# A linear-attention and squared-ReLU kernel: the planner's order replaced by a written table of steps

## The chip, the cores and the metric

One core of one Trainium2 chip runs the kernel. The metric is the device time of one execution in microseconds; below it is given as the median of three executions. The engines are TensorE (PE, with its weight loads PEld), VectorE (DVE), ScalarE (ACT), GpSimd (POOL) and SyncE (SP), which here only issues transfers.

## The reference

Four sequences (batch) of 768 tokens and 8 heads of 48 go through an attention with a decaying state, and its output, seen as 3072 tokens of 384, through two dense layers with a squared ReLU. r, k and v are 4 x 8 x 768 x 48, w and u 8 x 48, the weights 384 x 2048 and 2048 x 384, all in float32.

```python
for t in range(S):
    cur = np.einsum('bhd,bhe->bhde', u[None] * kt, vt)
    y[:, :, t] = np.einsum('bhd,bhde->bhe', rt, state + cur)
    state = w[None, :, :, None] * state + np.einsum('bhd,bhe->bhde', kt, vt)
...
h = np.maximum(x @ w_in, 0.0)
return (h * h @ w_out).astype(np.float32)
```

## The kernel before

The tokens are cut into 24 chunks of 128: chunk i is the piece i // 4 of sequence i % 4, so a state is handed on from chunk i to chunk i + 4. The work of a chunk is a chain of steps, and each step is one token of a list, such as `A12`. The engines run in the order of that list, each its own steps one after another. The steps of chunk i:

- `Lk`, `Lr`, `Lv` (SP, L593): the loads of k, r and v, 192 KB each, into eight buffers of each kind. `vb` (ACT, L635): v in bf16.
- `kh` (L606) and `rt` (L609): k and r times the powers of the decay, in bf16. `P0`, `P` (L614, L617), `du` (L621), `dv` (L631): the term with u. DVE or POOL run the products, `du` runs on DVE.
- The transposes of `kh` and `rt`: for the first chunks on PE (`Tk`, `Tr`, L641) with copies by ACT or DVE (`ek`, `er`, L602 and L603), for the later ones one transposing transfer `T` (SP, L662). `PE_T` is the first chunk that uses the transfer.
- `A` (PE, L672): the scores within the chunk, eight matmuls into two PSUM banks; `M` (DVE, L686): the mask, one instruction for each bank.
- `Y` (PE, L698 and L703): the output from the state and the masked scores; `U` (PE, L713) and `S` (DVE, L727 and L728): the new state; `xs` (DVE, L721): `Y` plus `dv`.
- The transpose of `xs`: on PE (`X`, L734) with a copy (`xT`) up to chunk `XD` - 1, from there a transposing transfer (`xT` on SP, L743).
- The dense layers work on units n, which are one chunk or a pair of chunks. `F` n_s (PE, L774): 12 matmuls of 128 columns for a single, 6 of 256 for a pair, into one bank; a single has four F steps, a pair eight. `R` (ACT, L787): ReLU out of PSUM. `Q` (L794 on ACT, L796 on POOL, L798 on DVE): the square; the one on DVE reads the bank once more, the others do not. `G` i_q (PE, L808): 4 matmuls of 384 columns, four G steps for a chunk. `os` (L819): the result out of PSUM; `st` (SP, L823): the store.
- The weights come in quarters, `W1_q` and `W2_q` (768 KB each, L758), with a cast `C1_q`, `C2_q` (L602) to bf16; `W2_3` comes by a transfer that POOL issues and that casts by itself (L760).
- At the start stand `wrow`, `urow` (loads of w and u), `ln`, `bw`, `exk`, `ext`, `bu`, `ub`, `wt`, `wl`, `wlm`, which make the powers of the decay and spread u over the partitions.

Every step of PE that takes a bank says which of the eight; a step that takes a bank again waits for the last reader of what lay in it. The `hr` tiles (R to Q) have four buffers, the `hq` tiles (Q to G) 32.

The order of the 915 steps comes from a planner, `make_plan` and `Plan.run`: every step has needs, costs by engine, a priority that follows from its due time with a period of 13 us for two chunks, and takes and gives banks. `run` plays them through with a model of the engines, of the transfer queues (`fluid`) and of the banks, always takes the step that can begin first, and writes down order, engine and bank. `MOVED` shifts single priorities by hand. At the end a loop walks through `order` and issues the steps; `plan.after` adds waits, such as a POOL step's wait for a DVE product that stands ahead of it.

Of the kernel before, what the change touches and what calls it, by code (L numbers as in the profile page):

```python
# [22 lines left out]
RING = 2.5
LANDING = 1.2
FILL = 8.0
FILL_GAP = 0.2
FILLED = False
FILL_UNTIL = 20.0
AHEAD = 2.8
TPA = 0.8  # L30
DVO = 0
MOVED = {
# [15 lines left out]
FLEX = 5
UB = -94.0
ST_SLACK = 5.0  # L50
W1GATE = [["Lv1"], ["Lv1"], ["Lv1"], ["Lv1"]]
W2GATE = [["Lv3"], ["Lk4"], ["Lv4"], ["Lk5"]]
HW1 = (0, 1, 2, 3)
HW2 = (0, 1, 2)
W1PRIO = (-93.5, -93.45, -92.4, -92.35)
W2PRIO = (-91.5, -91.4, -91.3, -91.2)
CASTS = ("ACT", "POOL")
XD = 18
WF = 5
LEAD = 3  # L60
SLACK = (1.0, 0.3, 0.5, 2.0)
LGATE = {6: ["W2_2"], 7: ["W2_3"]}
OPEN = {"kh": -6, "rt": 6, "P0": 8, "P": 10, "du": 4, "dv": 6, "S": 6}

# [9 lines left out]

class Plan:


    def __init__(self):
        self.steps = {}
        self.after = {}  # L80

    def add(self, key, eng, cost, needs=(), prio=0.0, lat=None, take=(), give=(), service=None,
            port=False, slack=0.0, ring=None, units=0.0):
        eng = (eng,) if isinstance(eng, str) else eng
        cost = cost if isinstance(cost, dict) else {e: cost for e in eng}
        self.steps[key] = dict(
            engs=eng, costs=cost, needs=[n for n in needs if n is not None],
            prio=prio + MOVED.get(key, 0.0),
            more=0.2 if lat is None else lat - max(cost.values()), take=take, give=give,
            service=service, port=port, slack=slack, ring=ring, units=units,  # L90
        )

    def fluid(self):
        key, queue, begin, service = self.jobs[-1]
        others = [self.span[j[0]][1] for j in self.jobs[:-1] if j[1] != queue]
        same = [self.span[j[0]][1] for j in self.jobs[:-1][::-1] if j[1] == queue][:1]
        begin = max([begin] + same)
        if not others or max(others) <= begin:
            self.span[key] = [begin, begin + service]
            return {key: self.span[key]}  # L100
        jobs = {q: [j for j in self.jobs if j[1] == q] for q in ("hw", "sw")}
        at = {"hw": 0, "sw": 0}
        left = {q: [j[3] for j in jobs[q]] for q in jobs}
        now = 0.0
        span = {}
        while any(at[q] < len(jobs[q]) for q in jobs):
            live = [q for q in jobs if at[q] < len(jobs[q]) and jobs[q][at[q]][2] <= now + 1e-9]
            coming = [jobs[q][at[q]][2] for q in jobs if at[q] < len(jobs[q]) and q not in live]
            if not live:
                now = min(coming)  # L110
                continue
            rate = {"hw": 1.0, "sw": 1.0} if len(live) == 1 else {"hw": 0.17, "sw": 0.83}
            step = min(left[q][at[q]] / rate[q] for q in live)
            if coming:
                step = min(step, min(coming) - now)
            for q in live:
                span.setdefault(jobs[q][at[q]][0], [now, now])
            now += step
            for q in live:
                left[q][at[q]] -= rate[q] * step  # L120
                if left[q][at[q]] <= 1e-9:
                    span[jobs[q][at[q]][0]][1] = now
                    at[q] += 1
        return span

    def room(self, at, units):

        spare = RING - units
        for key, q, _, _ in reversed(self.jobs):
            if q == "hw":  # L130
                a, b = self.span[key]
                u = self.steps[key]["units"]
                if u >= spare:
                    return max(at, b - (b - a) * spare / u)
                spare -= u
        return at

    def warm(self, at):
        return sum(max(0.0, b - max(a, at - 3.4)) for a, b in self.pe[-60:]) >= 2.0

    def fill(self, key, begin, end):

        if not self.steps[key]["take"] or begin > FILL_UNTIL:
            return 0, begin
        n = int(max(0.0, end - begin - FILL_GAP) * (FILL if begin > 4.0 else min(FILL, 4.5)))
        return n, self.dummies(n, begin)

    def dummies(self, n, begin):
        for _ in range(n):
            took = 0.107 if self.warm(begin) else 0.213  # L150
            self.pe.append((begin, begin + took))
            begin += took
        return begin

    def cost(self, key, eng, at):
        s = self.steps[key]
        c = s["costs"][eng]
        if eng == "PE" and not self.warm(at):
            c *= 1.75
        if s["port"] and eng == "DVE":  # L160
            c += max(0.0, self.free["POOL"] - at)
        if s["units"]:
            c = max(c, self.room(at + c, s["units"]) - at)
        return c

    def run(self, until=1e9):
        steps = self.steps
        free = self.free = {"SP": 0.5, "ACT": 1.8, "POOL": 2.8, "DVE": 1.5, "PE": 1.2}
        self.pe = []
        self.fills = {}  # L170
        self.jobs = []
        self.span = {}
        rings = {}
        done = self.done = {}
        self.start = {}
        self.took = {}
        self.eng = {}
        self.banks = {}
        bank_free = [0.0] * BANKS
        held = {}  # L180
        order = self.order = []
        caps = {"O": 4, "H": 4, "A": 5}
        lanes = []
        lock = None
        users = {}
        open_needs = {}
        for key, s in steps.items():
            open_needs[key] = len(set(s["needs"]))
            for n in set(s["needs"]):
                users.setdefault(n, []).append(key)  # L190
        place = {key: n for n, key in enumerate(steps)}
        todo = {key for key in steps if not open_needs[key]}
        while todo:
            taken = {b for h in held.values() for b in h[1]}
            spare = sorted((bank_free[b], b) for b in range(BANKS) if b not in taken)
            counts = {}
            for kind, banks in held.values():
                counts[kind] = counts.get(kind, 0) + len(banks)
            seen = {}
            for key in sorted(todo, key=place.get):  # L200
                s = steps[key]
                ready = max([done[n] for n in s["needs"]], default=0.0) + s["slack"]
                if s["take"]:
                    name, kind, count = s["take"]
                    if counts.get(kind, 0) + count > caps[kind]:
                        continue
# [680 lines left out]
```

## Time and profile before

| | us |
|---|---|
| median of three executions (176.71 to 177.4) | 176.97 |
| profiled execution | 176.04 |
| its span, first to last instruction | 174.0 |
| PE busy | 163.7 |
| PEld busy | 124.7 |
| DVE busy | 128.7 |
| ACT busy | 112.5 |
| POOL busy | 102.9 |

Busy times are sums over the span; the rest of an engine's span is waiting. A line of the chain of waits gives the start, the length and the work on which the end hung at that time; a line of the timeline gives start, length, engine, line, operation and tiles, and in brackets how long the engine had been idle and what released it. A landing time counts from the issue of a transfer to its completion.

### The profile page before, as it was taken

The numbers are of one execution on the slowest core, as the hardware profiler recorded it, in microseconds if no ns is written. First come the engines' busy times: TensorE is split into PE (matmuls) and PEld (weight loads), VectorE is DVE, ScalarE is ACT, GpSimd is POOL, SyncE is SP. The second block draws the span as 40 slices with busy tenths as digits, with TensorE's granted clock in tenths as the row PEclk, the third lists the DMA queues.
The fourth block names the chain that finished last, engine by engine and source line by source line (L and its number), as shares of the span: only waits on it lengthen the run. The fifth ranks groups of instructions, "written<-read, shape, count | busy, mean of one in ns | idle before, by whom it ended". The sixth has DMA issues, their size and how long they took to land.

```text
span 174.0 us, 4703 instructions
## 1 busy us (share of the span) xinstructions
PE 163.7 (94%) x1866; PEld 124.7 (72%) x1866; DVE 128.7 (74%) x238; ACT 112.5 (65%) x205; POOL 102.9 (59%) x121
## 2 busy tenths in 40 slices
PE   1979799999999999999999999999999999999992
PEld 1349688676887779967776867888776787866860
DVE  4698889589769499989699886999887269540620
ACT  4557899893795557946586743974784294743932
POOL 5022643249979998998999999969798200000000
PEclk9999999999999999999999999999999999999999
DMA  4999999999999799999799999999995621110302
GB/s 94 191 321 245 344 219 384 175 202 181 191 159 211 175 224 171 211 167 208 149 232 191 177 221 177 224 237 181 175 166 108 171 70 49 23 41 31 136 0 90
DMA packets 102520, 30.11 MB, mean 173 GB/s; under 512 B 95842, under 2 KB 100964, under 8 KB 102500
## 3 DMA queue, kind: packets, MB, share of 16 engines
q1 hardware_dynamic: 101972, 29.44, 84.6%
q0 software_dynamic: 528, 0.39, 1.8%
q8 instruction: 14, 0.23, 0.6%
q14 instruction: 6, 0.05, 0.1%
HBM read 20.45 MB, written 4.72 MB: 145 GB/s over the span
## 4 chain that ended last, share of the span: by engine, by line
PE 83%; DMA 8%; ACT 4%; SPq 3%; issue 1%; DVE 0%; ACTq 0%
PE ps_O L808 35%; PE ps_H L774 33%; DMA kf<-in_k_dram 5%; PE ps_A L672 4%; DMA vf<-in_v_dram 3%; PE ps_Y L703 2%; SPq L593 2%; PE ps_Y L698 2%; PE ps_U L713 2%; PE ps_X L734 2%; ACT W L602 1%; PE ps_wt L567 1%; ACT hr L787 1%; PE ps_Tk L641 1%; PE ps_Tr L641 0%
## 5 line engine op out<-in xcount | busy, mean ns | idle before, releaser
L774 PE MATMUL ps_H<-xT,W 128*128 128x128 bf16 (+1 forms) x816 | 72.8, 242 | 1.3 <-ACT W L602 1.1
L808 PE MATMUL ps_O<-W,hq 128*128 128x384 bf16 x384 | 71.9, 326 | 0.0
L787 ACT ACTIVATE hr<-ps_H 128x512 bf16<-128x512 f32 x96 | 56.3, 599 | 24.0 <-PE ps_H L774 22.0
L774 PEld LDWEIGHTS <-W 128*128 128x128 bf16 x816 | 60.2, 98 | 8.2 <-ACT W L602 1.2
L798 DVE TENSOR_TENSOR hq<-hr,ps_H 128x512 bf16<-128x512 bf16 x67 | 44.4, 681 | 19.0 <-ACT hr L787 18.8
L808 PEld LDWEIGHTS <-hq 128*128 128x128 bf16 x384 | 34.9, 98 | 18.6
L686 DVE TENSOR_TENSOR Bm<-ps_A,maskJT 128x512 bf16<-128x512 f32 x48 | 30.7, 681 | 2.3 <-PE ps_A L672 2.3
L614 POOL TENSOR_TENSOR P<-rf,kf 128x384 f32<-128x384 f32 x22 | 22.0, 998 | 12.3 <-DVE dv L631 7.6
L609 POOL TENSOR_TENSOR rk<-rf,Wt 128x384 bf16<-128x384 f32 x20 | 19.9, 998 | 3.5 <-DMA rf<-in_r_dram 2.9
L819 ACT COPY os<-ps_O 128x384 f32<-128x384 f32 x24 | 11.4, 477 | 14.5 <-PE ps_O L808 14.3
L617 POOL TENSOR_TENSOR P<-P,ub 128x384 f32<-128x384 f32 x20 | 19.9, 997 | 1.3
L631 POOL TENSOR_TENSOR dv<-vf,du 128x384 f32<-128x384 f32 x21 | 17.4, 828 | 5.4 <-DVE du L621 5.4
L606 POOL TENSOR_TENSOR rk<-kf,Wkhat 128x384 bf16<-128x384 f32 x19 | 19.0, 1000 | 1.3 <-DMA kf<-in_k_dram 1.1
L621 DVE TENSOR_REDUCE du<-P 128x8 f32<-128x384 f32 x24 | 13.1, 545 | 4.7 <-POOL P L617 4.7
L794 ACT ACTIVATE hq<-hr 128x512 bf16<-128x512 bf16 x25 | 15.7, 630 | 0.3
L721 DVE TENSOR_TENSOR xs<-ps_Y,dv 128x384 bf16<-128x384 f32 x24 | 13.2, 550 | 2.5 <-PE ps_Y L703 2.1
L635 ACT CAST vb<-vf 128x384 bf16<-128x384 f32 x24 | 12.2, 510 | 2.3 <-DMA vf<-in_v_dram 1.6
L602 ACT CAST W<-Wf 128x1536 bf16<-128x1536 f32 x7 | 10.3, 1477 | 2.1 <-DMA Wf<-in_moe_w_in_dram 1.3
L602 ACT COPY xT<-ps_X 128x384 bf16<-128x384 bf16 x14 | 6.7, 479 | 7.5 <-PE ps_X L734 7.5
L728 DVE TENSOR_TENSOR S0W<-ps_U,WLm 128x384 bf16<-128x384 f32 x20 | 11.1, 556 | 0.6
L703 PE MATMUL ps_Y<-vb,Bm 128*128 128x48 bf16 x192 | 11.5, 186 | 0.0
L672 PE MATMUL ps_A<-rkT 48*128 48x128 bf16 x192 | 9.8, 226 | 1.2 <-ACT rkT L602 1.2
(55 smaller groups left out, 117.0 us busy)
## 6 DMA issues: line engine op xcount, KB each, us to landing
kf<-in_k_dram SPq DMA_DIRECT2D x24, 192.0 KB, 4.5
rf<-in_r_dram SPq DMA_DIRECT2D x24, 192.0 KB, 4.2
vf<-in_v_dram SPq DMA_DIRECT2D x24, 192.0 KB, 4.5
out_dram<-os SPq DMA_DIRECT2D x24, 192.0 KB, 3.0
Wf<-in_moe_w_in_dram SPq DMA_DIRECT2D x4, 768.0 KB, 7.1
Wf<-in_moe_w_out_dram SPq DMA_DIRECT2D x3, 768.0 KB, 7.3
W<-in_moe_w_out_dram POOLq DMA_DIRECT2D x1, 384.0 KB, 5.9
rkT<-rk SPq DMA_TRANSPOSE x17, 4.0
```

What stands on the lines that cost most here:

```text
L602: return nc.scalar.copy(out, in_)
L606: return engine(f"kh{i}").tensor_mul(rk_buf[i % NK][:, 1, :, 0:D], nat["k", i], Wkhat)
L609: return engine(f"rt{i}").tensor_mul(rk_buf[i % NK][:, 0, :, 0:D], nat["r", i], Wt2)
L614: return engine(f"P0{i}").tensor_mul(P0, nat["r", i], nat["k", i])
L617: return engine(f"P{i}").tensor_mul(P0s[i], P0s[i], ub)
L631: return engine(f"dv{i}").tensor_mul(dv, nat["v", i], du_b)
L672: nc.tensor.matmul(Ap[e][:, hc, :], rkT[p0 : p0 + D, HP + hc, :], rkT[p0 : p0 + D, hc, :], start=True, stop=True, skip_group_check=True,)
L686: nc.vector.tensor_mul(Bm[:, e], Ap[e], mask_b)
L774: nc.tensor.matmul(hp[:, fi, :], W1[s // size][:, c, 128 * f : 128 * (f + 1)], xTs[n][:, :, c, :], start=(c == 0), stop=(c == CCH - 1), sk ...
L787: nc.scalar.activation(hr, hp, AF.Relu)
L798: nc.vector.tensor_mul(hq, hr, hp)
L808: nc.tensor.matmul(ps[f"O{i}"][:, 0:d_model], hsq[n, f // per][:, f % per, L * j : L * (j + 1)], W2[q][:, f % 4, :], start=(f == 0), stop= ...
```

## The change

The planner goes, with its costs, priorities and model. `ORDER` is a table of 921 tokens such as `A0:P34`: the step, the engine (P, A, D, G for POOL, S for SP) and the banks. `Plan.run` only reads it. The words that came with the change speak of 923 steps, searched one by one with a replayed model of the machine.

What else differs: chunks 5 and 6 are transposed by a transfer (`PE_T` 7 to 5, five chunks stay on PE), chunks 16 and 17 have their `xT` by a transfer (`XD` 18 to 16), chunks 22 and 23 are units of their own (`SINGLE_TAIL` 2). In PE's part of the table most scores stand in pairs, two A steps behind one another. Many products, squares and copies have another engine: 61 squares run on ACT (25 before), 22 on DVE (67), 13 on POOL (4); `os` is on DVE for 12 chunks; two weight casts are on POOL. The result of chunk 23 is copied in two halves, by ACT and DVE, and stored by two queues. A memset for a tile that was not used goes.

The diff, cut to its core (the table's first steps to `G0_1` and its last ones):

```diff
-PE_T = 7
-PERIOD = 13.0
-BANKS = 8
+PE_T = 5
+XD = 16
 SINGLE_HEAD = 10
-SINGLE_TAIL = 0
+SINGLE_TAIL = 2
 HQ = 32
...
+LOCKS = ("kh", "rt", "P0", "P", "dv", "C")
+ORDER = """
+Lr0:S wrow:S ln:A bw:P0 exk:A ext:A Lr1:S Lk0:S Lk1:S P00:D P01:D wt:P1 wl:A kh0:D kh1:D rt0:D
+urow:S Lr2:S bu:P0 ub:A Tk0:P1 ek0:A Lk2:S kh2:D Tr0:P2 rt1:D Lk3:S P02:D kh3:D rt2:D er0:A Tk2:P0
+Tr1:P1 er1:A Tk1:P2 ek1:A ek2:A A0:P34 Tk3:P1 A1:P25 Tr2:P0 Lr3:S Lv1:S Lv0:S vb0:A ek3:A vb1:A
+er2:A P0:D M0:D du0:D M1:D rt3:G P1:G Lv2:S W1_0:S du1:D Tr3:P6 er3:A vb2:A C1_0:A W1_1:S Lv3:S
+Lk4:S Lr4:S W1_2:S W1_3:S Lv4:S Lk5:S Lr5:S W2_0:S W2_1:S Lv5:S Lk6:S dv0:G P03:G dv1:G Y0:P3
+xs0:D U0:P4 U1:P1 A2:P07 M2:D Y1:P2 A3:P56 X0:P3 xs1:D X1:P0 xT0:A F0_0:P2 wlm:D P2:G P3:G du2:D
+du3:D dv2:G xT1:A F1_0:P0 Y2:P3 C1_1:A dv3:G kh4:G rt4:G vb3:A F1_1:P7 R1_0:A R0_0:A M3:D Y3:P5
+xs2:D U3:P0 U2:P6 X2:P3 F0_1:P2 S1:D xs3:D xT2:D X3:P5 Tk4:P1 S0:D F2_1:P3 Tr4:P4 xT3:D S2:D S3:D
+er4:D ek4:D F3_0:P5 F2_0:P6 F3_1:P0 Q1_0:A R1_1:A Q1_1:G P04:G P4:G R0_1:A Q0_1:D A4:P14 Q0_0:A
+C1_2:A F0_2:P7 F3_2:P2 R3_0:A Q3_0:D M4:D du4:D W2_3:G dv4:G kh5:G rt5:G T5:S C1_3:A F3_3:P5
+F2_3:P1 R3_1:A vb4:A Y4:P4 Q3_1:D R3_2:A Q3_2:D F0_3:P0 F1_2:P2 xs4:D X4:P4 R2_0:A R2_3:A Q2_0:D
+R2_1:A R0_2:A Q2_3:A xT4:A Q2_1:D F2_2:P1 W2_2:S R2_2:A R3_3:A Q0_2:A Q3_3:D F1_3:P6 R0_3:A Q2_2:A
+Q0_3:A F4_1:P4 vb5:A R4_1:A R1_3:A F4_3:P3 R4_3:A Q4_1:A R1_2:A C2_0:G U4:P3 F4_0:P7 S4:D G0_0:P0
+G3_0:P5 G2_0:P3 C2_1:G G3_1:P G0_1:P A5:P16 M5:D F4_2:P4 G1_0:P2 G2_1:P R4_0:A Q1_2:A Q4_0:A
...
+F17_1:P5 F17_0:P7 R16_0:A Q16_0:D R15_7:A Q15_4:A Q15_7:D R17_0:A R17_1:A G21_1:P F17_2:P6
+F16_1:P7 R16_1:A Q16_1:A F16_3:P5 R16_3:A Q16_3:A Q17_0:G Q17_1:G R16_2:A G21_2:P F17_3:P7 R17_3:A
+G22_0:P0 G20_2:P G22_1:P G21_3:P G23_0:P7 Q16_2:A R17_2:A Q17_3:A G22_2:P G23_1:P Q17_2:G G22_3:P
+st15:S os19:D st19:S st18:S os21:D os22:D G23_2:P st22:S st21:S G20_3:P os20:A st20:S G23_3:P
+os23:A sh23:A oh23:D st23:S
+"""
...
+    def run(self):
+        self.order, self.eng, self.banks, self.after = [], {}, {}, {}
         lock = None
...
+        for token in ORDER.split():
+            key, where = token.split(":")
+            self.order.append(key)
+            self.eng[key] = ENGINES[where[0]]
+            name = "H" + key[1:] if family(key) == "F" else "O" + key[1:-2] if family(key) == "G" else key
+            if where[1:]:
+                self.banks[name] = [int(b) for b in where[1:]]
+            if self.eng[key] == "DVE" and family(key) in LOCKS:
                 lock = key
+            elif self.eng[key] == "POOL":
+                self.after[key] = [lock] if lock else []
                 lock = None
+            if key[0] == "W" and self.eng[key] == "POOL":
+                self.after[key].append("Lk5")
+        return self.order
...
+        if i == N - 1:
+            nc.scalar.copy(t[:, 0:half], ps[f"O{i}"][:, 0:half])
+        else:
+            copy(f"os{i}", t, ps.pop(f"O{i}")[:, 0:d_model])
         osb[i] = t
 
+    def do_oh(i):
+        t = work.tile([128, H, D], FP32, name=f"oh_{i}", tag="P0").rearrange("p h d -> p (h d)")[:, 0:half]
+        nc.vector.tensor_copy(t, ps.pop(f"O{i}")[:, half:d_model])
+        osb[i, 1] = t
...
+    def do_sh(i):
+        return nc.scalar.dma_start(out=out_v[(i % B) * NCH + i // B][:, 0:half], in_=osb.pop(i)[:, 0:half])
```

More of the change, by code (lines that the diff above doesn't have):

```diff
@@ L16 @@
 NCH = 6
-PE_T = 7
-PERIOD = 13.0
-BANKS = 8
+PE_T = 5
+XD = 16
 SINGLE_HEAD = 10
-SINGLE_TAIL = 0
+SINGLE_TAIL = 2
 HQ = 32
[L23 to L32, printed above, removed]
[12 rows of a table removed]
-}
-LOOK = {"SP": 0.5, "POOL": 0.3}
-SQUARE = {(1, 1): "POOL", (1, 3): "DVE", (2, 0): "POOL", (2, 1): "ACT", (2, 2): "POOL", (2, 3): "DVE", (3, 0): "ACT", (3, 2): "ACT", (3, 3): "DVE", (4, 0): "ACT", (4, 1): "ACT", (4, 2): "ACT", (4, 3): "DVE", (5, 3): "POOL"}
@@ L48 @@
[L48 to L58, printed above, removed]
-WF = 5
[L60 to L63, printed above, removed]
+WF = 5
+ENGINES = {"P": "PE", "A": "ACT", "D": "DVE", "G": "POOL", "S": "SP"}
@@ new lines @@
+R2_1:A R0_2:A Q2_3:A xT4:A Q2_1:D F2_2:P1 W2_2:S R2_2:A R3_3:A Q0_2:A Q3_3:D F1_3:P6 R0_3:A Q2_2:A
+Q0_3:A F4_1:P4 vb5:A R4_1:A R1_3:A F4_3:P1 R4_3:A Q4_1:A R1_2:A C2_0:G U4:P3 F4_0:P7 S4:D G0_0:P0
+G3_0:P5 G2_0:P3 C2_1:G G3_1:P G0_1:P A5:P16 M5:D F4_2:P4 G1_0:P2 G2_1:P R4_0:A Q1_2:A Q4_0:A
+C2_2:A P05:G kh6:G P5:G du5:D dv5:D Lr6:S rt6:G U5:P1 Y5:P6 xs5:D S5:D G1_1:P G4_0:P7 G1_2:P
+G2_2:P Lr7:S Lk7:S X5:P1 G3_2:P G2_3:P Q1_3:A R4_2:A Q4_3:A os2:A xT5:D F5_0:P1 G3_3:P os3:A
+G0_2:P Lr8:S Lv6:S vb6:A F5_1:P3 T6:S A6:P54 Lk8:S rt7:G kh7:G T7:S rt8:D P06:D P6:D du6:D P07:G
@@ new lines @@
+Q7_3:A Q6_1:A st0:S Lr12:S Lv10:S rt10:G kh10:G T10:S rt11:G st1:S Lk12:S F8_2:P3 Q7_0:A R7_1:A
+R7_2:A G6_1:P P010:D kh11:D M9:D F8_1:P4 Y9:P0 U9:P2 F8_3:P5 R8_2:A Q7_2:A R8_1:A Q7_1:A G6_2:P
+G7_0:P3 vb10:A os5:A P10:D dv9:G du10:D xs9:D X9:P0 xT9:A R8_3:A T11:S Q8_2:A F8_0:P1 G7_1:P
+R8_0:A F9_2:P0 Lv11:S Lk14:S Lk13:S Lr13:S Lk15:S P011:G P11:G dv10:G os4:D Q8_1:D S9:D P012:D
+rt12:G st2:S Lv12:S st3:S kh12:G P12:G T12:S du11:D dv11:G rt13:G kh13:G P013:G A10:P52 M10:D
+A11:P47 M11:D R9_2:A F9_3:P1 F9_0:P0 G7_2:P vb11:A R9_3:A Q9_3:A Q8_3:A Q8_0:A U8:P1 F9_1:P2
@@ new lines @@
+R9_1:A R9_0:A Q9_0:A Y10:P4 S8:D xs10:D Y11:P7 xs11:D du12:D U11:P5 G7_3:P G6_3:P X10:P7 G8_0:P0
+X11:P4 Q9_2:A xT10:A xT11:A S11:D G9_0:P2 U10:P7 P13:D S10:D kh14:G dv12:D du13:D G8_1:P F10_7:P4
+F10_6:P5 F10_1:P7 T13:S Lr15:S R10_7:A kh15:G Q10_7:G rt15:G os7:A R10_1:A Q10_1:D Q9_1:A os6:D
+F10_0:P4 F10_2:P3 G8_2:P G9_1:P R10_0:A R10_2:A vb12:A st5:S Lr14:S P014:G P14:G Lv13:S dv13:G
+rt14:G Q10_2:D vb13:A A12:P64 A13:P71 M12:D M13:D R10_6:A Q10_6:A Q10_0:A G8_3:P G9_2:P F10_3:P3
+R10_3:A Q10_3:A G9_3:P Y12:P5 Y13:P1 os9:D xs12:D F10_5:P7 G11_0:P2 xs13:D X13:P1 X12:P5 xT12:D
@@ new lines @@
+Lk16:S st4:S Lr17:S st7:S F10_4:P3 G10_0:P4 U12:P5 xT13:D F11_2:P1 F11_3:P6 R10_4:A R10_5:A
+Q10_5:A R11_3:A Q10_4:A P015:G Lr16:S P016:D os8:D S12:D Q11_3:D du14:D rt16:G rt17:G P15:G du15:D
+Lv15:S Lv14:S vb14:A T14:S T15:S F11_1:P0 U13:P5 F11_7:P7 R11_1:A G11_1:P vb15:A F11_0:P6 G11_2:P
+G10_1:P R11_2:A Q11_2:A R11_0:A Lk17:S Lr18:S S13:D A14:P51 A15:P03 dv14:G P16:D kh16:G M14:D
+dv15:G Q11_1:A R11_7:A G10_2:P U15:P6 G11_3:P F11_5:P1 M15:D F11_4:P5 Y15:P0 Q11_7:D os11:D
+Q11_0:G kh17:G P017:G Y14:P3 xs14:D F11_6:P7 R11_6:A Q11_6:G G10_3:P X14:P3 U14:P2 xT14:A R11_5:A
@@ new lines @@
+R11_4:A xs15:D X15:P0 xT15:D du16:D G12_0:P7 G13_0:P3 F12_4:P1 G13_1:P F12_0:P5 Q11_4:A F12_1:P0
+R12_0:A st6:S st9:S Lk18:S Lr19:S Lv16:S Lk19:S kh19:G T16:S Lk21:S os10:A rt18:G S15:D S14:D
+rt19:D P17:D Q11_5:A R12_4:A vb16:A F12_3:P2 G12_1:P F12_2:P4 G12_2:P Q12_0:D kh18:G dv16:G T17:S
+Lv17:S st8:S A17:P56 Q12_4:D du17:D R12_3:A R12_1:A Lk20:S Lr20:S T18:S T19:S Lr21:S P018:D dv17:G
+P019:G kh20:G A16:P21 M16:D G13_2:P F12_5:P0 vb17:A R12_2:A U17:P4 G13_3:P U16:P1 F12_6:P2 Q12_3:A
+R12_5:A Q12_5:G P18:G Q12_1:A Q12_2:A Y16:P0 M17:D xs16:D Y17:P5 xs17:D S16:D S17:D G15_0:P6
@@ new lines @@
+G12_3:P G14_0:P5 F12_7:P0 G14_1:P G15_1:P os12:D R12_7:A Q12_7:A R12_6:A Q12_6:A os13:A A19:P07
+A18:P41 P020:G rt20:G G14_2:P G15_2:P xT16:S xT17:S F13_4:P2 R13_4:A F13_0:P3 R13_0:A Lv18:S
+rt21:D M18:D M19:D du18:D kh21:G P19:G du19:D Lv19:S P021:G dv18:G dv19:D Q13_4:G P20:G vb18:A
+vb19:A G14_3:P F13_3:P2 R13_3:A Q13_3:D F13_6:P3 U19:P0 Y19:P7 Y18:P1 xs18:D S19:D F13_1:P4
+G15_3:P U18:P1 F13_5:P2 R13_1:A Q13_0:A Q13_1:A R13_5:A F13_2:P0 R13_2:A Q13_2:A F13_7:P4 G17_0:P2
+G16_0:P0 S18:D xs19:D R13_6:A Q13_6:A T20:S T21:S st10:S st11:S os14:D os15:A G17_1:P A21:P35
@@ L72, in units @@
     )
-class Plan:
[L78 to L183, printed above, removed]
-        lock = None
[L185 to L206, printed above, removed]
-                    if kind != "H" and len(spare) - count < (0 if "H" in counts else 1):
-                        continue
-                    if len(spare) < count:
-                        continue
-                    ready = max(ready, spare[count - 1][0])
-                if s["ring"]:
-                    name, size, _ = s["ring"]
-                    held_by = rings.get(name, [])
-                    if len(held_by) >= size:
-                        if any(n not in done for n in held_by[-size]):
-                            continue
-                        ready = max([ready] + [done[n] for n in held_by[-size]])
-                if s["units"] and len(lanes) >= 8:
-                    ready = max(ready, done[lanes[-8]])
-                ends = []
-                for e in s["engs"]:
-                    at = max(free[e], ready)
-                    ends.append((at + self.cost(key, e, at), at, e))
-                _, at, e = min(ends)
-                seen.setdefault(e, []).append((at, s["prio"], place[key], key))
-            assert seen, ("stuck", sorted(todo)[:20], held)
-            best = None
-            for eng, c in seen.items():
-                first = min(c)[0]
-                pick = min((p, a, n, k) for a, p, n, k in c if a <= first + LOOK.get(eng, 0.0) + 1e-9)
-                if best is None or (pick[1], pick[0]) < (best[0], best[1]):
-                    best = (pick[1], pick[0], pick[3], eng)
-            at, _, key, eng = best
-            if at > until:
-                break
-            s = steps[key]
-            if eng == "PE":
-                self.fills[key], end = self.fill(key, free["PE"], at)
-                at = max(at, end)
-            took = self.cost(key, eng, at)
-            todo.remove(key)
-            for k in users.get(key, ()):
-                open_needs[k] -= 1
-                if not open_needs[k]:
-                    todo.add(k)
-            order.append(key)
-            self.start[key] = at
-            self.eng[key] = eng
-            self.took[key] = took
-            free[eng] = at + took
-            if eng == "PE":
-                if key[0] in "AFGUY":
-                    self.pe.append((at, at + took))
-            if s["port"] and eng == "DVE":
-                free["POOL"] = max(free["POOL"], at + took + 0.1)
@@ new lines, in family @@
+def family(key):
+    if key[0] in "CFRQGW" and "_" in key:
+        return key[0]
+    if key[:2] == "P0" and len(key) > 2:
+        return "P0"
+    return key.rstrip("0123456789")
+class Plan:
+    def run(self):
+        self.order, self.eng, self.banks, self.after = [], {}, {}, {}
+        lock = None
+        for token in ORDER.split():
[6 more added lines that the diff above has]
+            if self.eng[key] == "DVE" and family(key) in LOCKS:
@@ L257, in run @@
                 lock = key
-            elif eng == "POOL" and lock:
-                self.after[key] = list(self.after.get(key, ())) + [lock]
+            elif self.eng[key] == "POOL":
+                self.after[key] = [lock] if lock else []
                 lock = None
-            if s["ring"]:
-                rings.setdefault(s["ring"][0], []).append(s["ring"][2])
-            end = at + took + s["more"]
-            if s["service"]:
-                q = "sw" if eng == "POOL" else "hw"
-                if eng == "SP":
-                    lanes.append(key)
-                lead = 2.3 if q == "sw" else max(1.1, took if key[0] in "Tx" else took + 0.2 if s["units"] >= 1 else 0.0)
-                self.jobs.append((key, q, at + lead, s["service"]))
-                new = self.fluid()
-                self.span.update(new)
-                for k in new:
-                    done[k] = new[k][1] + LANDING
-            else:
-                done[key] = end
@@ L815, in do_G @@
             )
+    half = d_model // 2
     def do_os(i):
         t = work.tile([128, d_model], FP32, name=f"os_{i}", tag="os")
-        nc.scalar.copy(t, ps.pop(f"O{i}")[:, 0:d_model])
+        if i == N - 1:
+            nc.scalar.copy(t[:, 0:half], ps[f"O{i}"][:, 0:half])
+        else:
+            copy(f"os{i}", t, ps.pop(f"O{i}")[:, 0:d_model])
         osb[i] = t
+    def do_oh(i):
+        t = work.tile([128, H, D], FP32, name=f"oh_{i}", tag="P0").rearrange("p h d -> p (h d)")[:, 0:half]
+        nc.vector.tensor_copy(t, ps.pop(f"O{i}")[:, half:d_model])
+        osb[i, 1] = t
     def do_st(i):
-        return nc.sync.dma_start(out=out_v[(i % B) * NCH + i // B], in_=osb.pop(i))
+        to = out_v[(i % B) * NCH + i // B]
+        if i == N - 1:
+            return nc.sync.dma_start(out=to[:, half:], in_=osb.pop((i, 1)))
+        return nc.sync.dma_start(out=to, in_=osb.pop(i))
+    def do_sh(i):
+        return nc.scalar.dma_start(out=out_v[(i % B) * NCH + i // B][:, 0:half], in_=osb.pop(i)[:, 0:half])
     plain = {
@@ L836 @@
     for key in order:
-        if FILLED and plan.fills.get(key):
-            t = bank(plan.steps[key]["take"][0])
-            for _ in range(plan.fills[key]):
-                nc.tensor.matmul(t[:, 0:256], warm, warm_b, start=True, stop=True, skip_group_check=True)
         if key in plain:
@@ L850 @@
         else:
-            n = 2 if key[:2] == "P0" and len(key) > 2 else len(key.rstrip("0123456789"))
+            n = len(family(key))
             inst = one[key[:n]](int(key[n:]))
```

152 lines of the change are left out of this document (18 added, 134 removed), and 12 rows, old and new, of the table MOVED.

## The prediction

> **What bounds the kernel now.** I read the page first (span and busy times), then the busy times by stage, then the chain of waits in order of time, then the timeline of the opening with the landings of its transfers.
>
> ```profile
> span 174.0 us, 4703 instructions
> ...
> PE 163.7 (94%) x1866; PEld 124.7 (72%) x1866; DVE 128.7 (74%) x238; ACT 112.5 (65%) x205; POOL 102.9 (59%) x121
> ```
>
> The profiled execution took 176.04 us: 2.0 lie around its span of 174.0, and it is 0.9 below the median of 176.97. I work in shifts of the span and add them to the median. A measurement of this kernel can tell about 0.5% (0.9 us) from no change.
>
> ```profile
> 0.00:10.00 10.00, 5.97 (x28) 2.81 (x28) 5.76 (x18) 5.36 (x10) 2.29 (x14) 1.00 0.91 147
> ...
> 36.16:170.76 134.60, 134.57 (x1530) 102.02 (x1527) 101.05 (x177) 84.65 (x164) 90.92 (x97) 1.00 0.85 155
> ```
>
> Columns: stretch, its length, then busy PE, PEld, DVE, ACT, POOL. From 36.16 on PE has no pause at all (134.57 of 134.60) and every other engine has at least 33 us to spare. So there are three places to win or lose: PE's work after 36.16, one for one; how far the opening has got by then; and the 3.3 us after the last matmul. The chain gives the cost of each step on a PE that is never waiting:
>
> ```profile
> 35.93 0.22 PE ps_Tr L641 x4
> 36.16 0.67 PE ps_H L774 x12
> ...
> 70.04 0.17 PE ps_U L713 x4
> 70.21 1.34 PE ps_H L774 x24
> 71.55 0.17 PE ps_X L734 x3
> ...
> 75.03 0.33 PE ps_A L672 x8
> 75.36 0.76 PE ps_O L808 x4
> ...
> 142.59 0.55 PE ps_A L672 x16
> 143.14 0.76 PE ps_H L774 x6
> ...
> 160.29 5.24 PE ps_H L774 x48
> 165.53 5.21 PE ps_O L808 x32
> ...
> 170.76 0.48 ACT os L819
> ```
>
> An F step of a single chunk is 0.67, of a pair 5.24/8 = 0.655; a G step 5.21/8 = 0.65; a transpose of k or r 0.22, X 0.17, U 0.17. A score step A is 0.33, and the step behind it takes 0.76 in place of 0.65, so 0.44 in all. Two A steps in a row, which the kernel has once (142.59), are 0.55 + 0.11 = 0.66, so a pair saves 0.22. A Y step with a state is the time between these two rows, 0.37:
>
> ```profile
> 41.02 0.04 PE ps_Y L698
> ...
> 41.39 0.65 PE ps_O L808 x4
> ```
>
> **PE's work after the opening.** Tk, Tr of chunks 5 and 6 leave PE: 4 x 0.22 = 0.88. X of 16 and 17 leave it: 0.34. PE's part of the table has A steps side by side for 10/11, 12/13, 14/15, 16/17, 18/19, 20/21, 22/23: seven pairs against one, 6 x 0.22 = 1.32. Chunks 22 and 23 become single units: 8 x 0.67 - 8 x 0.655 = +0.12. Sum -2.4 us. The four transposes go to SP's queue instead (T5, T6, xT16, xT17); A5 is the first that needs one, at about 45 in the new order, and its transfer comes right behind Lk6 in the queue, so I cost it at nothing. Without that cover it costs one transfer of some 2 us, once.
>
> ACT takes over squares (61 in place of 25), DVE gives up 45 of them and takes os and prologue products, POOL gets lighter. By counts times durations ACT gains some 10 us over the whole; it had 50 to spare after 36.16, so nothing there.
>
> **The opening.** This is what decides. The new table puts eight loads of r and k, then three of v, in front of W1_0 (before: seven loads), and 17 loads and all of W1 in front of W2_0. The landings of before give the price of each transfer, since they come one behind the other on one queue:
>
> ```profile
> L593 SPq DMA_DIRECT2D kf<-in_k_dram x1: 419/419/419, 1.2 to 1.2; - x1
> DMA to landing us min/median/max: 3.0/3.0/3.0
> L593 SPq DMA_DIRECT2D kf<-in_k_dram x1: 706/706/706, 5.2 to 5.2; - x1
> ...
> DMA to landing us min/median/max: 4.4/4.4/4.4
> L758 SPq DMA_DIRECT2D Wf<-in_moe_w_in_dram x2: 487/617/747, 7.2 to 8.0; - x2
> ...
> DMA to landing us min/median/max: 5.8/6.6/7.4
> L593 SPq DMA_DIRECT2D rf<-in_r_dram x1: 892/892/892, 36.1 to 36.1; - x1
> ...
> DMA to landing us min/median/max: 4.6/4.6/4.6
> L593 SPq DMA_DIRECT2D vf<-in_v_dram x1: 1789/1789/1789, 37.1 to 37.1; - x1
> ...
> DMA to landing us min/median/max: 7.0/7.0/7.0
> ...
> W<-in_moe_w_out_dram POOLq DMA_DIRECT2D x1, 384.0 KB, 5.9
> ```
>
> Lk0 lands at 4.2 and Lk1, five loads later, at 9.6: 1.08 a load. W1_0 lands at 13.0, W1_1 at 15.4: 2.4 a weight quarter. Lr6 lands at 40.7 and the next, Lv6, at 44.1: 3.4 in place of 1.08, because W2_3, which POOL had issued at 37.1, moved beside it; it costs the queue 2.3.
>
> Now the new order. Its first load is issued at 0.8 in place of 1.2 (wrow goes second), so it lands near 3.8. W1_3 has 14 loads and three quarters in front of it: 3.8 + 13 x 1.08 + 4 x 2.4 = 27.4. Lv5 is best counted from Lv6 of before, which landed at 44.1 behind the same things and, besides, Lk6, Lr6, itself and W2_2: 44.1 - 3 x 1.08 - 2.4 - 0.4 = 38.1. (W2_3 is in it: POOL issues it when Lk5 lands, near 29, and 5.9 later it is done.)
>
> ACT runs in order, and each of its steps starts this long after the one ahead:
>
> ```profile
> 20.20 1.46 ACT L602 CAST W<-Wf 128x1536 bf16<-128x1536 f32 x1
> 21.57 0.60 ACT L787 ACTIVATE hr<-ps_H 128x512 bf16<-128x512 f32 x1
> ...
> 29.12 1.11 ACT L787 ACTIVATE hr<-ps_H 128x512 bf16<-128x512 f32 x2
> ...
> 47.49 1.14 ACT L794 ACTIVATE hq<-hr 128x512 bf16<-128x512 bf16 x2
> ...
> 53.59 0.50 ACT L635 CAST vb<-vf 128x384 bf16<-128x384 f32 x1
> 53.99 0.48 ACT L819 COPY os<-ps_O 128x384 f32<-128x384 f32 x1
> ```
>
> A cast 1.37, R 0.51, Q 0.51 to 0.54, vb 0.4; I take 0.4 for xT. From C1_3 at 27.4, the new order has on ACT nine R, four Q, vb4 and xT4 up to Q0_3: 1.4 + 4.6 + 2.2 + 0.8 = 9.0, so ACT is at vb5 by 36.4. There it waits for Lv5 until 38.1. Behind vb5 are queued R4_1, R1_3 and R4_3: R4_3 ends at 38.1 + 0.4 + 2 x 0.51 + 0.6 = 40.1. **Who waits for R4_3 is PE:** F4_3 writes bank 3, and the next step on PE, U4, writes bank 3 as well. PE gets F4_1 and F4_3 done by about 34.6 (xT4 ends near 33.3, then 2 x 0.67) and stands until 40.2. F4_0 and the first G steps are behind U4; G0_0 could have started no sooner than W2_0's landing (38.1 less Lv5 and W2_1, 34.6) and POOL's cast. That has no row: between ACT's 1.4 and the 4.0 of four such products (a cast reads one operand; I take 2), so near 37.
>
> ```profile
> L614 POOL TENSOR_TENSOR P<-rf,kf 128x384 f32<-128x384 f32 x22 | 22.0, 998 | 12.3 <-DVE dv L631 7.6
> ```
>
> State of PE when U4 starts at 40.2, against before at 36.16: done besides are F3_2, F3_3, F4_1, F4_3 (2.68), A4, Y4, X4 (0.98); not done are G0_0, G1_0, G2_0, G0_1, G1_1, G0_2 (3.91). Left to do: 134.6 - 3.66 + 3.91 - 2.4 = 132.4. PE ends at 172.6 in place of 170.76: **+1.9**.
>
> **PE's rate after the pause.**
>
> ```profile
> 15.91 1.44 PE ps_H L774 x12
> ...
> 18.34 1.35 PE ps_H L774 x24
> ...
> 21.73 1.51 PE L774 MATMUL ps_H<-xT,W 128*128 128x128 bf16 x24 [1.05 <-ACT W L602]
> ```
>
> The first F step takes 1.44 in place of 0.67, and the four steps from 15.91 to 18.34 take 2.43 where the prices above give 1.23: 1.2 lost on a PE that had been busy 6 of its first 10 us. A pause of 1.05 (before 21.73) costs nothing afterwards. A pause of 5.6 is not shown: 0 or 1.2. I take **+1.2**, since it is longer than any pause of the opening that had left PE slow. [...]
>
> **The end.** os23 becomes two halves on ACT and DVE, stored by two queues. The copy of 0.48 shrinks, the two transfers are half as long; 0 to -0.6, I take **-0.3**. ACT issues sh23 behind its own copy, nothing is queued there. Squares keep ahead of PE there: behind F17_3, ACT has two R and two Q left (2.2 us) up to Q17_3, PE ten G steps (6.5) up to G23_3, which reads it.
>
> Sum: +1.9 + 1.2 - 0.3 = +2.8. 176.97 + 2.8 = **179.8 us**; in the profiled execution 176.04 + 2.8 = 178.8. The late opening eats the 2.4 saved behind it and more.
>
> **Rivals.**
> (a) The pause in front of U4 is not there, because the loads come sooner than counted or the wait falls elsewhere; then the opening is worth what it was, and -2.4 - 0.3 gives 174.3. For it: PE has nothing else against it, and every saved step counts fully. Against: vb5, R4_3 and U4 stand in that order on their engines. It decides if U4 starts before 38.7, where PE's end comes out even.
> (b) W2_3 moves beside the queue without slowing it. Lv5 lands at 35.8, ACT alone sets R4_3 (36.4 + 2.0 = 38.4), PE's pause is 3.8: -0.2 to +1.0, 177.1. Against: the 3.4 us between Lr6 and Lv6.
> (c) Worse: after the opening PE waits as well.
>
> ```profile
> L686 DVE TENSOR_TENSOR Bm<-ps_A,maskJT 128x512 bf16<-128x512 f32 x48 | 30.7, 681 | 2.3 <-PE ps_A L672 2.3
> ```
>
> An A pair holds four of eight banks until DVE has made both masks, 4 x 0.68 us; if PE waits 0.5 at each of seven pairs, 3.5 more: 183.3. Against: before, one pair passes without a gap (142.59).
> (d) The pair saves nothing (its 0.55 was chance): +1.3, 181.1.
>
> **Chances.** Forecast 0.46, (a) 0.21, (b) 0.15, (c) 0.10, (d) 0.08. The forecast's own range is 178.2 to 181.8: no cold price below, a load late by 1 us and a later wait of 1 us above. The whole range 174.8 to 183.0 leaves out the better half of (a) and most of (c). Faster by over 0.5%: (a) and a little of (b), 0.24; within: most of (b), 0.12; slower 0.64.
>
> **What the changed profile would show.** Right: vf of chunk 5 landing at 38 and ACT's vb waiting for it; PE idle some 5 us up to 40 with ACT's hr as the releaser of ps_U; twelve-matmul F steps at over 1 us just after; then a gapless PE to about 174; A groups of 16 matmuls at 0.55. Wrong: PE gapless from 30 on (then a), or gaps spread over 60 to 150 (then c).

## The result, and the profile after

The changed kernel is faster: 175.73 us against 177.25 (medians of 21 executions each), ratio 0.9909, 95% interval 0.9884 to 0.9933. The prediction said 179.8 us and slower, so it was wrong in direction. A second set of executions of the same kernel (label `c_after` below) gave 0.9914. The ratios compare runs taken side by side and leave out runs marked slow, so they differ a little from the quotient of the medians.

One correction comes ahead of everything else. The diff as it is printed above has one wrong character, and the prediction stands on it: the token reads `F4_3:P1` in the changed kernel, not `F4_3:P3`. It was copied wrongly and then reasoned from. In the kernel that was timed, F4_3 writes bank 1, and U4, on bank 3, does not wait for R4_3. The next step on PE that takes bank 1 is the score step A5 (`A5:P16`, banks 1 and 6). Also, the two step counts above stand the wrong way round: the planner's order has 921 steps, the table 915 tokens.

The profiled execution of the changed kernel took 176.71 us with a span of 175.0. That is the slowest of its 21, while the profiled one of before (176.04) is faster than all 21 of before (lowest 176.37). The two spans therefore show +1.0 where the medians show -1.5, and I compare the parts of the traces, not their ends. The page of the changed kernel:

```profile
span 175.0 us, 4726 instructions
...
PE 162.5 (93%) x1892; PEld 126.4 (72%) x1892; DVE 118.9 (68%) x223; ACT 118.3 (68%) x221; POOL 98.7 (56%) x114
```

The stretch from U4 to PE's last matmul (its length, then busy PE, PEld, DVE, ACT, POOL):

```profile
36.09:171.51 135.42, 132.90 (x1512) 101.10 (x1509) 91.55 (x165) 92.20 (x177) 78.29 (x81) 1.00 0.81 162
```

U4 starts at 36.09. The prediction's list of what is done there holds, and 132.4 us of PE work should be left. PE ends at 171.51, 135.4 later: 3.0 us more than the work, of which 2.5 are idle time in this row (135.42 less 132.90). Before, 134.57 of 134.60 us were busy. The pauses in the timeline (start, length, engine, line, tiles, in brackets the idle time ahead of it and its releaser):

```profile
36.09 0.33 PE L435 MATMUL ps_U<-vb,rk 128*128 128x96 bf16 x4
36.26 0.83 PE L496 MATMUL ps_H<-xT,W 128*128 128x128 bf16 x12
36.93 3.41 PE L530 MATMUL ps_O<-W,hq 128*128 128x384 bf16 x20
41.70 0.40 PE L394 MATMUL ps_A<-rkT 48*128 48x128 bf16 x8 [1.35 <-ACT hr L509]
...
46.42 1.46 PE L530 MATMUL ps_O<-W,hq 128*128 128x384 bf16 x8 [0.41 <-ACT W L324]
...
140.10 0.20 PE L420 MATMUL ps_Y<-S0W,rkT 128*128 128x96 bf16 x1 [0.75 <-ACT hr L509]
```

U4 has no pause in front of it. The first one stands in front of A5 (41.70), then G1_2 waits for the cast C2_2, then Y21 for the bank of H14_4. A bracket counts from the end that the profile models for the step ahead: the five G steps last 3.41 in their row, where 5 x 0.65 is 3.25. So each pause costs some 0.17 more than its bracket, and three times that is the other 0.5 of the 3.0. A5 has three things to wait for: the transfer T5, bank 6, which R1_3 frees, and bank 1, which R4_3 frees. R1_3 and R4_3 are the second and the third step behind vb5 on ACT (T5's issue with its landing time, then ACT's timeline):

```profile
L384 SPq DMA_TRANSPOSE rkT<-rk x1: 5937/5937/5937, 33.6 to 33.6; - x1
...
DMA to landing us min/median/max: 7.8/7.8/7.8
```

```profile
39.66 0.51 ACT L357 CAST vb<-vf 128x384 bf16<-128x384 f32 x1 [2.26 <-DMA vf<-in_v_dram]
40.08 1.56 ACT L509 ACTIVATE hr<-ps_H 128x512 bf16<-128x512 f32 x3
```

T5 lands at 33.6 + 7.8 = 41.4. vb5 waits 2.26 for its load, and the three R behind it are R4_1, R1_3 and R4_3: the third ends at 40.08 + 1.56 = 41.64, and A5 starts 0.06 later. So the bracket names the right engine, and the step is R4_3: the wait that the prediction put in front of U4 stands in front of A5, and T5 is over some 0.2 earlier.

### The profile page after: what moved, and what is told of

Same layout as the page of the kernel before. It is cut to its first block, busy times and chain, and to the rows that moved or that the text cites. A ratio compares the mean times of both kernels' runs of the same rounds, so it can differ in the third digit from the quotient of the medians.

```text
span 175.0 us, 4726 instructions
## 1 busy us (share of the span) xinstructions
PE 162.5 (93%) x1892; PEld 126.4 (72%) x1892; DVE 118.9 (68%) x223; ACT 118.3 (68%) x221; POOL 98.7 (56%) x114
## 4 chain that ended last, share of the span: by engine, by line
PE 68%; DMA 14%; SPq 7%; ACT 4%; DVE 3%; issue 2%; POOL 1%; ACTq 0%; DVEq 0%
PE ps_O L530 31%; PE ps_H L496 28%; DMA Wf<-in_moe_w_out_dram 8%; SPq L315 6%; DMA Wf<-in_moe_w_in_dram 3%; PE ps_A L394 3%; DMA vf<-in_v_dram 2%; PE ps_Y L425 2%; ACT W L324 2%; PE ps_Y L420 2%; PE ps_U L435 2%; PE ps_X L456 1%; ACT hr L509 1%; POOL W L325 1%; DVE ps_U L449 1%
## 5 line engine op out<-in xcount | busy, mean ns | idle before, releaser
L496 PEld LDWEIGHTS <-W 128*128 128x128 bf16 x864 | 62.7, 100 | 7.2 <-ACT W L324 0.5
L516 ACT ACTIVATE hq<-hr 128x512 bf16<-128x512 bf16 x61 | 37.1, 629 | 0.6
L331 POOL TENSOR_TENSOR rk<-rf,Wt 128x384 bf16<-128x384 f32 x17 | 16.9, 998 | 22.8 <-DMA rf<-in_r_dram 11.0
L518 POOL TENSOR_TENSOR hq<-hr 128x512 bf16<-128x512 bf16 x13 | 13.8, 1064 | 21.2 <-ACT hr L509 21.2
L520 DVE TENSOR_TENSOR hq<-hr,ps_H 128x512 bf16<-128x512 bf16 x22 | 14.7, 682 | 10.9 <-ACT hr L509 10.9
L353 POOL TENSOR_TENSOR dv<-vf,du 128x384 f32<-128x384 f32 x17 | 14.0, 830 | 6.3 <-DVE P L339 2.6
L336 POOL TENSOR_TENSOR P<-rf,kf 128x384 f32<-128x384 f32 x13 | 13.0, 1000 | 2.1 <-DVE P L339 1.6
L325 DVE COPY os<-ps_O 128x384 f32<-128x384 f32 x12 | 6.6, 551 | 8.7 <-PE ps_O L530 8.7
L425 PEld LDWEIGHTS <-Bm 128*128 128x128 bf16 x192 | 9.7, 99 | 1.4 <-issue 0.8
L336 DVE TENSOR_TENSOR P<-rf,kf 128x384 f32<-128x384 f32 x11 | 7.8, 713 | 3.8 <-DMA kf<-in_k_dram 3.8
```

The lines of the kernel that those rows point to most:

```text
L331: return engine(f"rt{i}").tensor_mul(rk_buf[i % NK][:, 0, :, 0:D], nat["r", i], Wt2)
L336: return engine(f"P0{i}").tensor_mul(P0, nat["r", i], nat["k", i])
L353: return engine(f"dv{i}").tensor_mul(dv, nat["v", i], du_b)
L425: nc.tensor.matmul(Y[:, hc, D * e : D * (e + 1)], Bm[:, e, hc, :], vb[:, 2 * hc + e, :], start=(c == 0), stop=True, skip_group_check=True,)
L496: nc.tensor.matmul(hp[:, fi, :], W1[s // size][:, c, 128 * f : 128 * (f + 1)], xTs[n][:, :, c, :], start=(c == 0), stop=(c == CCH - 1), sk ...
L516: nc.scalar.square(hq, hr)
```

## The experiments

All ratios are to the kernel before on the same chip, with 95% intervals. The kernels are the changed kernel with the edit shown, unless said otherwise.

**The changed kernel again.**

> The changed kernel once more, for a second profiled execution. Work theory (the gain is PE work saved, 2.4 us, and 0.3 at the end, less new PE pauses): ratio 0.99 again, and where this execution is shorter than the 175.0 span, PE's pauses after 36 us sum to less than the 2.5 of the first profile, by the same amount. Rival, filling theory (the gain is in the opening, the steps saved lie beside other waits): the two executions differ in the time at which U4 and F4_0 start, not in later pauses.

Measured: 175.45 us, ratio 0.9914 (0.9882 to 0.9947). Span 174.6, PE's end at 171.12. U4 starts later here (36.44), and PE's pauses after it sum to 1.8 in place of 2.5:

```profile
41.08 0.40 PE L394 MATMUL ps_A<-rkT 48*128 48x128 bf16 x8 [0.39 <-ACT hr L509]
...
139.71 0.20 PE L420 MATMUL ps_Y<-S0W,rkT 128*128 128x96 bf16 x1 [1.02 <-ACT hr L509]
```

The pause in front of A5 is 0.96 shorter. 0.35 of it is the later opening, which the wait takes up; the rest is the load of v5, which lets vb5 start at 39.04 in place of 39.66. A5 starts 2.04 after vb5 in both traces. PE's end is 0.4 sooner although U4 is later, which speaks for the work theory.

**The token that the prediction had read.**

```diff
-F4_3:P1
+F4_3:P3
```

> One token: F4_3 on bank 3 in place of bank 1, which is what the prediction had read. Prediction's mechanism: U4 waits for R4_3, which ends near 41.5 behind vb5; PE stands from about 36 to 41.6, the pause of 1.4 in front of A5 goes into it: +4.2 against the changed kernel, +5.4 if PE is slow afterwards; 180 to 181 us, ratio to before 1.015 to 1.022. Rival (the step list has room to give this back later): under +1.5, ratio below 1.0.

Measured: 180.68 us, ratio 1.0198 (1.0147 to 1.0249).

```profile
41.45 0.48 PE L435 MATMUL ps_U<-vb,rk 128*128 128x96 bf16 x4 [5.89 <-ACT hr L509]
41.73 1.48 PE L496 MATMUL ps_H<-xT,W 128*128 128x128 bf16 x12
43.01 4.82 PE L530 MATMUL ps_O<-W,hq 128*128 128x384 bf16 x20
47.77 0.40 PE L394 MATMUL ps_A<-rkT 48*128 48x128 bf16 x8
```

This is the kernel that the prediction was about, and its mechanism is shown: U4 waits 5.89 for R4_3 (forecast 5.6), and the same U4, F4_0 and five G steps take 41.45 to 47.77, 6.3, where the changed kernel needs 4.26 without its pause. The slow rate after the pause costs 2.1 us (1.2 was taken). The granted clock on its page shows it (40 slices of 4.5 us, tenths of full speed; the 5 is the slice from 40.4 to 44.9):

```profile
PEclk9999999985899999999999999999999999999999
```

In the trace's clock record the half clock lasts from 39.04, 3.5 us after PE stopped, to 45.87, 4.4 us after it went on; the mean over 30 to 40 us is 0.95. One digit in a table of 915 tokens is worth 2.9% here. Five of the six executions lie between 180.6 and 181.5, one is at 178.42; what was different in that one was not looked at.

**What A5 waits for: three kernels.** vb5 later on ACT; chunk 5 transposed on PE; both.

```diff
 e_vb5, and in e_both too:
-vb5:A R4_1:A R1_3:A F4_3:P1 R4_3:A Q4_1:A R1_2:A
+R4_1:A R1_3:A F4_3:P1 R4_3:A Q4_1:A R1_2:A vb5:A
 e_t5pe, and in e_both too:
-T5:S
...
-G0_0:P0 G3_0:P5 G2_0:P3 C2_1:G G3_1:P G0_1:P
+G0_0:P0 Tk5:P3 ek5:D G3_0:P5 C2_1:G Tr5:P3 er5:D G3_1:P G2_0:P3 G0_1:P
```

> The cast vb5 moved four steps back on ACT, behind R1_2, so that R4_1, R1_3, R4_3 do not wait for the load of v5. ACT theory (A5 stood because R1_3 held its bank): A5 starts near 40.4 in place of 41.7, -1.3 us, ratio 0.983. Transfer theory (A5 stood because T5 landed at 41.4): A5 still at 41.4 to 41.7, 0 to -0.3, ratio 0.99.

> Chunk 5 transposed on PE again (Tk5, Tr5, copies on DVE), T5 off SP's queue. PE work +0.44. Transfer theory: A5 no longer waits for T5, and W2_2 is issued 6 us sooner, so C2_2 does not hold G1_2: -1.4 - 0.4 + 0.4, about -1.4, ratio 0.983. ACT theory: A5 still waits for R1_3 behind vb5 until 41.2 or more: 0 to -0.4 in all, ratio 0.99.

> Chunk 5 transposed on PE and vb5 behind R1_2. If A5 waits for whichever is later of T5's landing and R1_3, then either alone leaves a rest and both together remove the pause: A5 follows the G steps without idle time, about -0.8 against e_t5pe, ratio 0.984. If C2_2, which now waits behind a later ACT queue, takes the place: a pause of 0.4 to 1 in front of G1_2, ratio 0.988.

Measured: e_vb5 175.34 us, 0.9917 (0.9883 to 0.9951); e_t5pe 174.76 us, 0.9887 (0.9856 to 0.9918); e_both 173.46 us, 0.9837 (0.981 to 0.9865). The first step on A5, in e_vb5 and then in e_t5pe:

```profile
40.79 0.40 PE L394 MATMUL ps_A<-rkT 48*128 48x128 bf16 x8 [0.32 <-DMA rkT<-rk]
```

```profile
41.35 0.40 PE L394 MATMUL ps_A<-rkT 48*128 48x128 bf16 x8 [0.74 <-ACT hr L509]
```

With vb5 out of the way A5 waits for T5; with T5 out of the way it waits for ACT, and again the third R behind vb5, R4_3, ends 0.06 before it. The expectations name R1_3 and its bank 6; it is R4_3 and bank 1. The edit frees both, so the test holds for either. In all six traces in which vb5 stands ahead of R4_3 and its load is late (the changed kernel twice, e_f43, e_t5pe, and below e_nopairs and w_after), PE goes on 2.03 or 2.04 us after vb5 starts: at A5, in e_f43 at U4. So neither theory alone is right: the two waits end nearly together, and taking one away shows the other. e_vb5 gains nothing that shows; its A5 starts at 40.79, between the two forecasts. e_t5pe gains 0.7 us by the medians, with overlapping intervals; in its trace the pause in front of G1_2 is gone too, as forecast. Both edits together give what was forecast, 0.984. In e_both PE has no pause from U4 to its end:

```profile
34.76:167.90 133.14, 133.12 (x1520) 101.30 (x1517) 90.20 (x167) 92.03 (x177) 78.24 (x81) 1.00 0.85 163
```

133.1 us of work are left at U4. The prediction's sum gives 132.4, and 0.44 for Tk5 and Tr5, together 132.84: the saved work was sized to 0.3 here.

**The pairs.**

```diff
-A10:P52 M10:D A11:P47 M11:D R9_2:A F9_3:P1
+A10:P52 M10:D F9_3:P1 A11:P47 M11:D R9_2:A
 (and so at 12/13, 14/15, 16/17, 18/19, 22/23)
```

> The changed kernel with six of its seven score pairs split: the PE step that stood behind the pair now stands between its two A steps (all but 20/21). Work theory: each split costs 0.22, +1.3 us, ratio 0.991 + 0.007 = 0.998, and no group of 16 score matmuls but one is left in the trace. Rival (the chain's 0.44 for a lone A is partly an artefact of modelled ends, pairs save nothing): 0 to +0.3, ratio 0.991 to 0.993.

Measured: 176.14 us, ratio 0.9978 (0.9945 to 1.001), 0.0064 above c_after or 1.1 us; the two intervals overlap a little. PE's work settles the size better: from U4 (35.46) to its last matmul (170.94) PE is busy 134.18, against 132.90 in the changed kernel, both with three pauses. Chain of the changed kernel, then of e_nopairs:

```profile
75.54 0.55 PE ps_A L394 x16
```

```profile
99.88 0.33 PE ps_A L394 x8
100.21 0.76 PE ps_O L530 x4
100.97 0.33 PE ps_A L394 x8
```

The 0.55 of a pair and the 0.76 behind a lone A are there as costed. Six pairs are worth 1.28 us of PE's work, and 1.3 was forecast.

**The end alone, on the kernel before.**

```diff
+            nc.scalar.copy(t[:, 0:half], ps[f"O{i}"][:, 0:half])
+            nc.scalar.dma_start(out=..., in_=t[:, 0:half])
...
+            nc.vector.tensor_copy(t2, ps.pop(f"O{i}")[:, half:d_model])
...
+        return nc.sync.dma_start(out=to[:, half:] if i == N - 1 else to, in_=osb.pop(i))
```

> The kernel before with only the end changed: os23 in two halves on ACT and DVE, stored by ACT's and SP's queue. Work theory: from the last matmul to the end 3.3 becomes 3.0, ratio 0.998 (0.997 to 1.0). Rival (the halves follow one another, because DVE waits for ACT's copy out of the same bank, and only the transfer is shorter): the same ratio but DVE's half starts at the end of ACT's. The profile is also a second execution of the order before: its PE end tells whether 170.7 was typical.

Measured: 176.59 us, ratio 1.0012 (0.998 to 1.0044): no gain that shows; the forecast 0.998 is the edge of the interval.

```profile
171.44 0.32 ACT L822 COPY os<-ps_O 128x192 f32<-128x192 f32 x1 [0.17 <-PE ps_O L808]
171.78 0.37 ACTq L823 DMA_DIRECT2D out_dram<-os  x1
171.79 0.36 DVE L825 COPY oh<-ps_O 128x192 f32<-128x192 f32 x1 [4.60 <-ACT os L822]
172.17 0.33 SPq L833 DMA_DIRECT2D out_dram<-oh  x1
```

DVE's half starts when ACT's ends, as the rival said, and 0.32 + 0.36 is more than the 0.48 of the whole copy. Whether the program orders the two or the hardware does is not told apart. From the last matmul to the end it is 3.4 here, 3.5 in the changed kernel, 3.3 before. In this execution of the order before PE ended at 171.41, 0.7 later than in the one profiled first.

**The late v loads near 140 us.**

```diff
-R14_1:A vb20:A R13_7:A
+R14_1:A R13_7:A vb20:A
-vb21:A ... R14_4:A
+... R14_4:A vb21:A
-Lv20:S Lr23:S Lv21:S
+Lv20:S Lv21:S Lr23:S
```

> e_both, and vb20 behind R13_7, vb21 behind R14_4, Lv21 ahead of Lr23. The pause of 0.75 to 1.0 near 140 us (Y21 waiting for R14_4, which stands behind vb21 and its load) goes: PE without a pause over 0.2 from 46 on, ratio 0.980. If the pause only shows in some executions, as e_vb5 and e_t5pe had none: 0.984.

Measured: 173.69 us, ratio 0.985 (0.9822 to 0.9879), not to be told from e_both, which has no pause there either. The pause near 140 shows in both traces of the changed kernel (0.75, 1.02) and as 0.23 in e_nopairs, and not in e_vb5, e_t5pe and e_both, whose order there is the same; nothing is gained by the edit.

**The rate of the opening.** Executions of the same code differ between 18 and 24 us. In the profiles of the changed kernel and c_after the first 24 matmuls of F take 2.72, in e_both 1.50, though the three are alike up to there. Six extra matmuls on PE in front of F0_0 (their result is not used), on the changed kernel and on e_both, and e_both again:

```diff
+        if key == "F0_0":
...
+            for _ in range(6):
+                nc.tensor.matmul(t[:, 0:256], warm[:, 0:128], warm, start=True, stop=True, skip_group_check=True)
```

> The changed kernel with six extra matmuls of 256 columns on PE in front of F0_0, in the wait for xT1 (their result is not used). Pause theory: the first F steps run at full rate, U4 starts near 35 in place of 36.1 to 36.4, but A5 waits for T5 and R1_3 all the same, so the pause in front of it grows by what the opening gains: ratio 0.990 (0.987 to 0.993). Clock theory (the opening's rate sets the end): -1.3 us, ratio 0.983.

> e_both with the same six matmuls. Pause theory: no wait stands behind the opening now, so what the opening gains reaches the end; where e_both already had a fast opening nothing changes: ratio 0.983 (0.981 to 0.985), and no run over 174.5. If the matmuls stand in F0_0's way: up to +0.6, ratio 0.987.

> e_both once more. Pause theory: ratio 0.984 again; if this execution's first F steps run at half rate (24 matmuls in 2.7 in place of 1.5), U4 starts 1.3 later and PE ends 1.3 later than 167.9, with no pause in between that takes it up.

Measured: w_after 175.04 us, 0.9895 (0.9868 to 0.9921); w_both 174.12 us, 0.9844 (0.9813 to 0.9874); c_both 174.05 us, 0.9844 (0.9811 to 0.9877). In w_after the extra matmuls did not do what they were meant to: F still began at half rate (24 matmuls in 2.72), U4 at 35.82, and A5 paused 1.26, so this run does not tell the two theories apart. In w_both F began at full rate (1.50), with U4 at 35.73; one of its four executions took 174.75, over the 174.5 that was given as the limit. c_both tells them apart: its opening was slow, e_both's was fast (two lines of each, c_both first).

```profile
19.59 2.72 PE L496 MATMUL ps_H<-xT,W 128*128 128x128 bf16 x24 [0.96 <-ACT xT L324]
...
36.47 0.33 PE L435 MATMUL ps_U<-vb,rk 128*128 128x96 bf16 x4
```

```profile
18.25 1.50 PE L496 MATMUL ps_H<-xT,W 128*128 128x128 bf16 x24 [0.35 <-ACT xT L324]
...
34.76 0.33 PE L435 MATMUL ps_U<-vb,rk 128*128 128x96 bf16 x4
```

U4 is 1.7 later and PE's end 2.2 later (170.10 against 167.90; 1.3 was forecast for both): without the wait in front of A5 the opening reaches the end. The four traces without that wait agree: U4 starts at 34.76 (e_both), 35.17 (e_best), 35.73 (w_both) and 36.47 (c_both), and PE ends 133.1, 133.1, 133.1 and 133.6 later. The rate of the first F steps is only a part of when U4 starts: e_best took 2.72 for them too.

e_both is the version that beats both kernels: 0.9837 and, the second time, 0.9844.

## Why the prediction was wrong, by its own steps

- **What bounds the kernel** held: PE after the opening, one for one. e_both's gapless 133.1 us and e_nopairs' 1.28 us of added work are this accounting.
- **PE's work, -2.4**: held to 0.3 by the sum over the rest of e_both's trace (0.6 in c_both's). Of its parts only the pairs were tried alone; the transposes and the single units were not.
- **"F4_3 writes bank 3, and the next step on PE, U4, writes bank 3 as well"**: this is the step that failed. It is a misread token; the bank is 1. PE does wait for R4_3, but at A5, with 4.26 us of work in between, so 1.35 us are left of a pause of 5.89. With the token as it was read, the kernel takes 180.68 us, against the 179.8 forecast and inside its own range of 178.2 to 181.8. The argument was right for another kernel, and low in size: U4 starts 1.25 later than forecast there, and the slow rate costs 0.9 more.
- **Lv5 at 38.1, ACT waiting for it at vb5**: the wait is there, and vb5 started at 39.66 (39.04 in c_after), after ACT had waited 2.26 (it was at vb5 by 37.4, forecast 36.4). The transfer of W2_3 was sized from 5.9 us between issue and landing; here it took 9.5. That this held up Lv5 was not tried.
- **T5 "at nothing", with some 2 us if the cover is gone**: the cover was the misread pause. Without it A5 is due at 40.35 and starts at 41.70, behind T5 (41.4) and R4_3 (41.64). R4_3 alone explains the start; T5 shows where R4_3 is early, as a pause of 0.32 in e_vb5. So T5 was a term put at nothing that is due as soon as the other wait goes, though not at the 2 us named.
- **+1.2 for PE's rate after the pause**: the changed kernel has no such pause. No row of before shows the rate after one of that length; the 1.2 was an estimate from the slow start of the opening. e_f43, which has the pause, shows 2.1, with a granted clock of 0.50 from 39.04 to 45.87: 5.89 us idle, then 1.48 for an F step that took 0.83 in the changed kernel. A low clock came without such a pause as well: in the opening of the changed kernel it fell to 0.50 at 17.6 us, and PE's longest pause from 14.2 to 24.5 was 0.96 (last section).
- **The end, -0.3**: no gain that shows (b_tail). That DVE's half would start only when ACT's ends (171.79 against 171.44 + 0.32 there) was overlooked.
- **Rivals**: (a), no pause, came nearest with 174.3; the kernel is about halfway between it and no change. Its sign, U4 before 38.7, came true, but its PE without a pause did not: pauses of 1.8 to 2.5 us in the profiled executions take back most of the 2.4. (The start of U4 at which PE's end comes out even is 170.76 - 132.4 = 38.4; 38.7 holds only with the 0.3 of the end.) (d) fell with e_nopairs. (b) had Lv5 at 35.8, and it came at 39.7; (c) had PE waiting after the opening, and it does, but not at the pairs, where (c) put it.

The median is 1.5 us below before, while the two profiled traces add up to +0.8 at PE's end. An execution of the order before with 171.41, and the range of the changed kernel's 21 runs (174.29 to 176.71), are enough to span the difference; how long the pauses are in its median execution was not measured. 0.3 of the 1.5 lie outside the span: the time is 1.72 longer than the span in the median of the changed kernel's executions (1.67 to 1.89 in all 21) and 2.0 longer in those of before (1.84 to 2.15). The prediction kept the 2.0. The split end is not the cause, since b_tail has 2.06; the cause stays open.
